# Reordering a dense unit: five products between uses of bank X, shrink's steps in three gaps, transforms in the first and fourth

## The chip, the cores and the metric

The kernel runs on one core of a Trainium2 chip. The metric is the device time in microseconds (us) of one execution, lower is better. All runs told of here are in the fast state (granted TensorE clock 0.984 to 0.99 over the span).

## The reference

```python
def _attn_ref(x, filt_r, filt_i):            # x (8, 3008, 256), filters (1505, 256)
    X = np.fft.rfft(x, axis=1)
    return np.fft.irfft(X * (filt_r + 1j * filt_i)[None], n=x.shape[1], axis=1)

def _moe_ref(x, w_in, w_out):                # x (24064, 256), w_in (256, 2048), w_out (2048, 256)
    h = x @ w_in
    return (h - np.tanh(h)) @ w_out
```

## The kernel before

The Fourier transforms are matrix products ("transforms": pf, pz, pe, pu), run for one batch while the dense layers of the batch before are computed. Each 2x2 block product of the dense layers is done with seven products and some sums in place of eight. The work is cut into 192 **dense units**, in five stages, 0 to 4, of 24, 48, 48, 48 and 24 units. Unit U runs three things at once: `up` of U (14 products into banks X, Y, Z), `shrink` of U-1 (the nonlinear part, on ScalarE and VectorE), and `down` of U-2 (14 products into four accumulator banks o0 to o3). The seven carry the numbers 1 to 7; each has two halves, and each half counts as one of the 14. Every fourth unit ends an accumulation, and `down` then also forms the output sums. There are four stretches between uses of bank X in a unit; I call them gaps one to four. In the program, `d()` issues `down`'s next products, `e()` its next sums, `s()` shrink's next step, `t(k)` one transform step if one is due.

```python
# up(U): the order of a unit
mm(X, 1, True); mm(Y, 2, True)
s1 = copied("s1")                            # ScalarE copies X
t(0); d(); s()
V.tensor_add(h[:, 0, :, 0:w], Y, s1)
e(); s(); s(); t(1)
mm(X, 6, False); mm(Z, 5, True)
u2 = copied("u2")
d(); s(); e(); t(2)
mm(X, 7, False)
u3 = copied("u3")
V.tensor_add(h[:, 3, :, 0:w], Z, u3)         # h3
d(); s(); e(); t(3)
mm(X, 4, False)
V.tensor_copy(h[:, 2, :, 0:w], X)            # h2: frees X for the next unit
s(); d(); e(); t(4)
mm(Z, 3, False)
V.tensor_add(h[:, 1, :, 0:w], Z, u2)

# shrink(U): 2 stands for h2 and h3, 0 for h0 and h1
def start(k):
    ACT.activation(y[k], ht[k], AF.Arctan, scale=S)
    ACT.activation(y[k], y[k], AF.Square)
def square(k):
    V.tensor_mul(ht[k], ht[k], y[k])
    ACT.activation(sq[k], y[k], AF.Square, bias=near_b, scale=A)
def end(k):
    V.scalar_tensor_tensor(out=ht[k], in0=sq[k], scalar=K, in1=ht[k], ...)
start(2); yield; square(2); yield; end(2); yield; start(0); yield; square(0); yield
end(0); combine(...)                         # four sums on GpSimd
yield

# down(U): two products share each accumulator bank
at = {1: (0, 0), 2: (0, 1), 3: (1, 0), 5: (1, 1), 6: (2, 0), 7: (2, 1), 4: (3, 0)}
mm(1, 2); yield                              # both halves k of both products
if done: ACT.copy(p1, product(1)); V.tensor_add(o[:, 0, 0:w], product(2), p1)
yield
mm(3, 5); yield
if done: ACT.copy(p5, product(5)); V.tensor_add(x12, product(3), p5)
yield
mm(6, 7); yield
if done: V.tensor_add(u2, product(6), p1); V.tensor_add(p1, product(7), u2); ...
yield
mm(4); yield
if done: ...
# ... (cut: transforms, loads and stores, weights, the exact fallback)
```

Of the kernel before, what the change touches and what calls it, by code (L numbers as in the profile page):

```python
# [143 lines left out]
def kernel(  # L144
# [9 lines left out]
    nc = tc.nc  # L154
    V, G, ACT = nc.vector, nc.gpsimd, nc.scalar
# [13 lines left out]
    def dram(t, off, dims):  # L169
        return bass.AP(tensor=t, offset=off, ap=[list(d) for d in dims])  # L170
# [19 lines left out]
    wd = cst.tile([128, 7, DFF // 2], F32, name="wd")  # L190
# [271 lines left out]
    def combine(b, t, shared=False):  # L462
        G.tensor_sub(t[0], b[0][1], b[0][0])  # L463
        G.tensor_sub(t[1], b[1][1], t[0])  # L464
        (V if shared else G).tensor_sub(t[2], b[1][1], b[0][1])  # L465
        G.tensor_sub(t[3], t[1], b[1][0])  # L466
# [4 lines left out]
    def up(U, d, e, s, t):  # L471

        i, u = divmod(U, 4)
        b, tu, w = uts[i]
        rhs = [b[0][0], b[1][0], b[1][1], tu[:, 3, 0:w], tu[:, 0, 0:w], tu[:, 1, 0:w],
               tu[:, 2, 0:w]]
        banks = {k: ps.tile([128, 2, 256], F32, tag=k, bufs=1, name=k) for k in "xyz"}
        X, Y, Z = (banks[k][:, :, 0:w] for k in "xyz")
        h = dn.tile([128, 4, 2, 256], F32, tag="h", bufs=3, name="h")
        hs[U] = (h, w)  # L480

        def mm(bank, q, first):
            for k in range(2):
                nc.tensor.matmul(bank[:, k], wu[:, q - 1, (2 * u + k) * 128:(2 * u + k + 1) * 128],  # L484
                                 rhs[q - 1], start=(first and k == 0), stop=True,
                                 skip_group_check=True)

        def copied(tag):
            t = dn.tile([128, 2, 256], F32, tag=tag, bufs=1, name=tag)[:, :, 0:w]
            ACT.copy(t, X)  # L490
            return t


        mm(X, 1, True)
        mm(Y, 2, True)
        s1 = copied("s1")
        t(0)
        d()
        s()
        V.tensor_add(h[:, 0, :, 0:w], Y, s1)  # L500
        e()
        s()
        s()
        t(1)
        mm(X, 6, False)
        mm(Z, 5, True)
        u2 = copied("u2")
        d()
        s()
        e()  # L510
        t(2)
        mm(X, 7, False)
        u3 = copied("u3")
        V.tensor_add(h[:, 3, :, 0:w], Z, u3)
        d()
        s()
        e()
        t(3)
        mm(X, 4, False)
        V.tensor_copy(h[:, 2, :, 0:w], X)  # L520
        s()
        d()
        e()
        t(4)
        mm(Z, 3, False)
        V.tensor_add(h[:, 1, :, 0:w], Z, u2)

    def shrink(U):

        h, w = hs.pop(U)  # L530
        ht = {k: h[:, k:k + 2].rearrange("p a b n -> p (a b) n")[:, :, 0:w] for k in (0, 2)}

        def tiles(tag, bufs):
            return dn.tile([128, 4, 256], F32, tag=tag, bufs=bufs, name=tag)[:, :, 0:w]

        y, sq = {}, {}

        def start(k):
            y[k] = tiles("y", 2)
            ACT.activation(y[k], ht[k], AF.Arctan, scale=S)  # L540
            ACT.activation(y[k], y[k], AF.Square)  # L541

        def square(k):
            sq[k] = tiles("sq", 1)
# [4 lines that stand above are left out]
            V.scalar_tensor_tensor(out=ht[k], in0=sq[k], scalar=K, in1=ht[k],  # L549
                                   op0=ALU.add, op1=ALU.mult)  # L550

        start(2)
        yield
        square(2)
        yield
        end(2)
        yield
        start(0)
        yield
        square(0)  # L560
        yield
        end(0)
        t = dn.tile([128, 4, 2, 256], F32, tag="t", bufs=2, name="t")
        blocks = [[h[:, 2 * a + k, :, 0:w] for k in range(2)] for a in range(2)]
        combine(blocks, [t[:, k, :, 0:w] for k in range(4)], U + 1 == 4 * len(groups))
        gs[U] = (blocks, t, w)
        yield
# [3 lines left out]
    def down(U):  # L571


        i, u = divmod(U, 4)
        b, t, w = gs.pop(U)
        rhs = [b[0][0], b[1][0], b[1][1], t[:, 3, :, 0:w], t[:, 0, :, 0:w], t[:, 1, :, 0:w],
               t[:, 2, :, 0:w]]
        if u == 0:
            accs[i] = [ps.tile([128, 2, 256], F32, tag=f"o{k}", bufs=1, name=f"o{k}")
                       for k in range(4)]  # L580
        acc = accs[i]
        at = {1: (0, 0), 2: (0, 1), 3: (1, 0), 5: (1, 1), 6: (2, 0), 7: (2, 1), 4: (3, 0)}

        def product(q):
            bank, k = at[q]
            return acc[bank][:, k, 0:w]

        def mm(*qs):
            for k in range(2):
                for q in qs:  # L590
                    nc.tensor.matmul(product(q), wd[:, q - 1, (2 * u + k) * 128:  # L591
                                                    (2 * u + k + 1) * 128],
                                     rhs[q - 1][:, k], start=(u == 0 and k == 0 and q == qs[0]),
                                     stop=(u == 3 and k == 1), skip_group_check=True)

        done = u == 3
        if done:
            p1, p5, u2, x12 = (dn.tile([128, 256], F32, tag=k, bufs=1, name=k)[:, 0:w]
                               for k in ("p1", "p5", "pu2", "x12"))
            o = dn.tile([128, 2, CH * 128], F32, tag="o", bufs=1, name="o")  # L600
        mm(1, 2)
        yield
        if done:
            ACT.copy(p1, product(1))
            V.tensor_add(o[:, 0, 0:w], product(2), p1)
        yield
        mm(3, 5)
        yield
        if done:
            ACT.copy(p5, product(5))  # L610
            V.tensor_add(x12, product(3), p5)
        yield
        mm(6, 7)
        yield
        if done:
            V.tensor_add(u2, product(6), p1)
            V.tensor_add(p1, product(7), u2)
            G.tensor_add(o[:, 0, w:2 * w], u2, x12)
        yield
        mm(4)  # L620
        yield
        if done:
            V.tensor_add(o[:, 1, 0:w], product(4), p1)
            G.tensor_add(o[:, 1, w:2 * w], p1, p5)
            accs.pop(i)
            if i + 1 < len(groups):
                stores.append((i, o))
            else:
                store_last(i, o)
        yield  # L630
# [162 lines left out]
    with tc.tile_pool(name="tr", bufs=2) as tr:  # L793
        with tc.tile_pool(name="pro", bufs=1) as pro, \
# [103 lines left out]
            with tc.manual_schedule():  # L898
# [43 lines left out]
                for j in range(NK // 2):  # L942
# [7 lines left out]
                    for i in range(2):  # L950
                        k = (2 * j + i) % 4
# [26 lines left out]
        with tc.tile_pool(name="dn", bufs=2) as dn, \  # L978
# [34 lines left out]
            with tc.manual_schedule():  # L1013
# [3 lines left out]
                for U in range(total + 2):  # L1017
                    i, u = divmod(U, 4)
                    if U < total:
                        p, c = groups[i]  # L1020
                        if c == 0 and u == 0:
                            units = 4 * len(CHUNKS[p])
                            steps, done = [], 0 if p else EARLY
                            if p + 1 < len(UNITS):
                                n_f = len(chunks_of(UNITS[p + 1], XH))
                                n_m = 2 * NK // (3 - len(UNITS[p + 1]))
                                steps = [0.01 * units + 1.36 * units * (k - done) / (n_f - done)
                                         for k in range(n_f)]
# [16 lines left out]
                    def d():  # L1045

                        next(dw, None)

                    def e():

                        next(dw, None)

                    def s():

                        next(sh, None)

                    def t(k):


                        nonlocal ms, done  # L1060
                        if k == 2 and stores:
                            store(*stores.pop())
                        store_some(4)
                        if U >= total:
                            return
                        pos = 20 * c + 5 * u + k
                        if u == 3 and k in (0, 2) and i + 1 < len(groups):
                            next(lasts)
                        elif done < len(steps) and steps[done] <= pos:
                            if done < n_f:  # L1070
                                next(fs)
                            else:
                                next(ms)
                            done += 1
                            if done == n_f:
                                ms = middle(p + 1, z1)
                                next(ms)
                        if i == len(groups) - 1 and U + 2 < total and k != 1:
                            next(bounds)
                        if k in (0, 2, 4):  # L1080
                            next(late, None)
                        elif U > 0:
                            next(copies, None)
# [56 lines left out]
```

## Time and profile before

| | before |
|---|---|
| time | 2852.15 us, median of 5 runs (2849.91 to 2857.07) |
| TensorE busy | 96% of the span |
| VectorE, ScalarE, GpSimd busy | 70, 66, 61% |
| start losses of TensorE after the prologue | 98.9 us of 2730 |

The **start loss** is by how much a record on TensorE starts later than usual after the one before it, put down to the product that starts late. The prediction below works it out and shows the lines.

In the profile's lines PE is TensorE, PEld its weight loads, DVE VectorE, ACT ScalarE and POOL GpSimd; L514 is line 514 of the kernel. Shrink's `square` and `end` are L545 and L549 before, L547 and L551 after; h3 is L514 and L513, h2 L520 and L519.

### The profile page before, as it was taken

Reading aid. Unit: us, or ns where it says so; the run is one execution under the profiler, and the core shown is the slowest. Engines: PE = TensorE matmul, PEld = TensorE weight load, DVE = VectorE, ACT = ScalarE, POOL = GpSimd, SP = SyncE. Lnnn points to the kernel's source line nnn. Section 1 sums busy time; section 2 is a strip of 40 time slices with the busy share of each in tenths; the row PEclk is TensorE's granted clock in tenths of the full one; section 3 lists DMA queues with packets and bytes.
Section 4 is the critical chain, followed back from the end, with each engine's and each line's share of the span. In section 5 each row is a group of like instructions: output and inputs, shape, how many; then the busy total and the mean of one; then the engine's idle time right before and its main releaser. Section 6 shows DMA issues by size and latency. Waiting matters only on the chain.

```text
span 2850.8 us, 36441 instructions
## 1 busy us (share of the span) xinstructions
PE 2744.0 (96%) x12482; PEld 2276.7 (80%) x12482; DVE 1983.7 (70%) x2211; ACT 1871.5 (66%) x2450; POOL 1738.0 (61%) x1381
## 2 busy tenths in 40 slices
PE   5789999999999999999999999999999999999998
PEld 2567777888878887888877788788888888898887
DVE  4675666766766777766776777676687777777876
ACT  3655666666666666666666667666666666666665
POOL 4345777544677767644576776755466666555554
PEclk7989999999999999999999999999999999999999
DMA  9644443232223322132232223212222322111010
GB/s 265 190 152 118 113 113 92 60 93 84 73 67 80 85 73 59 41 98 78 67 99 67 70 71 83 53 39 68 58 65 62 78 55 57 30 19 25 16 22 16
DMA packets 324269, 217.53 MB, mean 76 GB/s; under 512 B 225037, under 2 KB 276485, under 8 KB 323882
## 3 DMA queue, kind: packets, MB, share of 16 engines
q1 hardware_dynamic: 269304, 160.36, 23.1%
q10 hardware_dynamic: 52818, 51.53, 6.0%
q0 software_dynamic: 1952, 3.22, 0.5%
q8 instruction: 100, 1.64, 0.2%
q14 instruction: 95, 0.78, 0.1%
HBM read 138.87 MB, written 79.17 MB: 76 GB/s over the span
## 4 chain that ended last, share of the span: by engine, by line
PE 77%; ACT 8%; DVE 6%; issue 3%; DMA 3%; POOL 1%; SPq 1%; ACTq 1%; DVEq 0%; POOLq 0%
PE o L591 31%; PE x L484 20%; PE z L484 9%; PE y L484 5%; PE pe L365 3%; PE pu L448 3%; PE pz L384 3%; ACT y L540 2%; PE pf L305 2%; DVE h L545 2%; ACT y L541 1%; DVE uv L399 1%; ACT zs L398 1%; ACT u L490 1%; DMA filt<-in_filt_i_dram 1%
## 5 line engine op out<-in xcount | busy, mean ns | idle before, releaser
L591 PE MATMUL o<-t,wd 128*128 128x256 f32 (+2 forms) x3072 | 775.8, 375 | 0.0
L545 DVE TENSOR_TENSOR h<-h,y 128x1024 f32<-128x1024 f32 (+2 forms) x384 | 582.1, 1516 | 258.1 <-ACT y L541 258.1
L591 PEld LDWEIGHTS o<-t,wd 128*128 128x128 f32 x3072 | 580.6, 190 | 71.7
L484 PE MATMUL x<-tu,wu 128*128 128x256 f32 (+2 forms) x2304 | 591.6, 379 | 18.4 <-ACT u L490 16.9
L549 DVE SCALAR_TENSOR_TENSOR h<-sq,h 128x1024 f32<-128x1024 f32 (+2 forms) x384 | 569.9, 1484 | 20.8 <-ACT y L540 0.5
L463 POOL TENSOR_TENSOR t<-h 128x512 f32<-128x512 f32 (+2 forms) x192 | 240.7, 1253 | 558.9 <-DVE h L549 495.9
L591 PE MATMUL o<-h,wd 128*128 128x256 f32 (+2 forms) x2304 | 581.1, 375 | 0.2 <-DVE h L549 0.2
L484 PEld LDWEIGHTS x<-tu,wu 128*128 128x128 f32 x2304 | 429.4, 191 | 161.5 <-issue 73.3
L591 PEld LDWEIGHTS o<-h,wd 128*128 128x128 f32 x2304 | 430.9, 190 | 70.9 <-issue 19.1
L546 ACT ACTIVATE sq<-y,near_b 128x1024 f32<-128x1024 f32 (+2 forms) x384 | 435.4, 1134 | 6.1 <-DVE h L549 1.4
L540 ACT ACTIVATE y<-h 128x1024 f32<-128x1024 f32 (+2 forms) x384 | 400.0, 1042 | 14.8 <-ACT e L368 7.6
L541 ACT ACTIVATE y<-y 128x1024 f32<-128x1024 f32 (+2 forms) x384 | 399.3, 1040 | 12.2
L490 ACT COPY s<-x 128x512 f32<-128x512 f32 (+2 forms) x192 | 110.8, 577 | 439.8 <-PE x L484 431.2
L466 POOL TENSOR_TENSOR t<-t,h 128x512 f32<-128x512 f32 (+2 forms) x192 | 308.8, 1608 | 0.1
L490 ACT COPY u<-x 128x512 f32<-128x512 f32 (+2 forms) x384 | 219.4, 571 | 68.6 <-PE x L484 33.3
L464 POOL TENSOR_TENSOR t<-h,t 128x512 f32<-128x512 f32 (+2 forms) x192 | 241.7, 1259 | 15.1
L465 POOL TENSOR_TENSOR t<-h 128x512 f32<-128x512 f32 (+2 forms) x191 | 250.2, 1310 | 0.0
L400 POOL TENSOR_TENSOR zs<-zs,ft 128x512 f32<-128x512 f32 x112 | 165.9, 1481 | 117.4 <-ACT zs L398 117.3
L401 POOL TENSOR_TENSOR uv<-uv,zs 128x512 f32<-128x512 f32 x112 | 214.9, 1919 | 15.6 <-DVE uv L399 7.2
L484 PE MATMUL x<-ut,wu 128*128 128x256 f32 (+2 forms) x768 | 198.8, 381 | 8.1 <-DVE h L520 6.5
L500 DVE TENSOR_TENSOR h<-y,s 128x512 f32<-128x512 f32 (+2 forms) x192 | 130.2, 678 | 96.2 <-PE y L484 86.0
L484 PE MATMUL z<-tu,wu 128*128 128x256 f32 (+2 forms) x768 | 194.5, 376 | 0.1
(120 smaller groups left out, 3289.1 us busy)
## 6 DMA issues: line engine op xcount, KB each, us to landing
a<-ct SPq DMA_DIRECT2D x64, 384.0 KB
ct<-e ACTq DMA_DIRECT2D x128, 192.0 KB
ft<-filt SPq DMA_DIRECT2D x96, 256.0 KB
out_dram<-ot SPq DMA_DIRECT2D x1392, 16.0 KB
ct<-a ACTq DMA_DIRECT2D x80, 256.0 KB
x_sb<-in_x_dram SPq DMA_DIRECT2D x69, 256.0 KB
e<-ct SPq DMA_DIRECT2D x33, 512.0 KB
fg<-fg SPq DMA_DIRECT2D x40, 392.0 KB
```

The source lines that it names most:

```text
L463: G.tensor_sub(t[0], b[0][1], b[0][0])
L464: G.tensor_sub(t[1], b[1][1], t[0])
L465: (V if shared else G).tensor_sub(t[2], b[1][1], b[0][1])
L466: G.tensor_sub(t[3], t[1], b[1][0])
L484: nc.tensor.matmul(bank[:, k], wu[:, q - 1, (2 * u + k) * 128:(2 * u + k + 1) * 128], rhs[q - 1], start=(first and k == 0), stop=True, ski ...
L490: ACT.copy(t, X)
L540: ACT.activation(y[k], ht[k], AF.Arctan, scale=S)
L541: ACT.activation(y[k], y[k], AF.Square)
L545: V.tensor_mul(ht[k], ht[k], y[k])
L546: ACT.activation(sq[k], y[k], AF.Square, bias=near_b, scale=A)
L549: V.scalar_tensor_tensor(out=ht[k], in0=sq[k], scalar=K, in1=ht[k], op0=ALU.add, op1=ALU.mult)
L591: nc.tensor.matmul(product(q), wd[:, q - 1, (2 * u + k) * 128: (2 * u + k + 1) * 128], rhs[q - 1][:, k], start=(u == 0 and k == 0 and q == ...
```

## The change

The intent: bank X is used four times a unit, with 6, 6, 4 and 4 products between the uses. The two short gaps made TensorE wait for the copies out of X. The change makes all four gaps five products long by cutting `down` into groups of 3, 3, 5 and 3, gives each gap its share of shrink, and from stage 1 on keeps transforms out of gaps two and three (but for one pu in every fourth unit), so that they don't stand before u2, u3 and h2. The core of the diff:

```diff
         mm(X, 1, True)
-        mm(Y, 2, True)
         s1 = copied("s1")
+        mm(Y, 2, True)
         t(0); d(); s()
         V.tensor_add(h[:, 0, :, 0:w], Y, s1)
         e()
-        s(); s(); t(1)
         mm(X, 6, False)
-        mm(Z, 5, True)
         u2 = copied("u2")
-        d(); s(); e(); t(2)
+        mm(Z, 5, True)
+        t(1); d(); s(); e()
         mm(X, 7, False)
         u3 = copied("u3")
         V.tensor_add(h[:, 3, :, 0:w], Z, u3)
-        d(); s(); e(); t(3)
+        t(2); d(); s(); e()
         mm(X, 4, False)
         V.tensor_copy(h[:, 2, :, 0:w], X)
-        s(); d(); e(); t(4)
+        t(3); s(); d(); e()
         mm(Z, 3, False)
         V.tensor_add(h[:, 1, :, 0:w], Z, u2)
+        t(4)
 # shrink (start(k) is cut into turn(k), the arctan, and power(k), the square)
-        start(2); yield; square(2); yield; end(2); yield; start(0); yield; square(0); yield
+        turn(2); power(2); yield
+        square(2); turn(0); yield
+        end(2); power(0); square(0); yield
         end(0); combine(...)
 # down
-        mm(1, 2); yield
+        mm((1, 0), (2, 0), (1, 1)); yield
         if done: ACT.copy(p1, product(1))
-                 V.tensor_add(o[:, 0, 0:w], product(2), p1)
         yield
-        mm(3, 5); yield
+        mm((2, 1), (3, 0), (3, 1)); yield
+        if done: V.tensor_add(o[:, 0, 0:w], product(2), p1)
+        yield
+        mm((5, 0), (6, 0), (5, 1), (6, 1), (7, 0)); yield
         if done: ACT.copy(p5, product(5))
+                 V.tensor_add(u2, product(6), p1)
                  V.tensor_add(x12, product(3), p5)
+                 G.tensor_add(o[:, 0, w:2 * w], u2, x12)
         yield
-        mm(6, 7); yield
-        if done: V.tensor_add(u2, product(6), p1); V.tensor_add(p1, product(7), u2); G.tensor_add(...)
-        yield
-        mm(4); yield
-        if done: ...
+        mm((7, 1), (4, 0), (4, 1)); yield
+        if done: V.tensor_add(p1, product(7), u2); ...
 # places of transforms
-        elif done < len(steps) and steps[done] <= pos:
+        elif (p == 0 or k in (0, 3, 4)) and done < len(steps) and steps[done] <= pos:
```

More of the change, by code (lines that the diff above doesn't have):

```diff
@@ L494, in up @@
         mm(X, 1, True)
+        s1 = copied("s1")
         mm(Y, 2, True)
-        s1 = copied("s1")
         t(0)
@@ L501, in up @@
         e()
-        s()
-        s()
-        t(1)
-        mm(X, 6, False)
-        mm(Z, 5, True)
-        u2 = copied("u2")
+        mm(X, 6, False)
+        u2 = copied("u2")
+        mm(Z, 5, True)
+        t(1)
         d()
@@ L510, in up @@
         e()
-        t(2)
         mm(X, 7, False)
@@ L514, in up @@
         V.tensor_add(h[:, 3, :, 0:w], Z, u3)
+        t(2)
         d()
@@ L517, in up @@
         e()
-        t(3)
         mm(X, 4, False)
         V.tensor_copy(h[:, 2, :, 0:w], X)
+        t(3)
         s()
@@ L523, in up @@
         e()
-        t(4)
         mm(Z, 3, False)
         V.tensor_add(h[:, 1, :, 0:w], Z, u2)
+        t(4)
     def shrink(U):
@@ L536, in shrink, with turn, power @@
         y, sq = {}, {}
-        def start(k):
+        def turn(k):
             y[k] = tiles("y", 2)
             ACT.activation(y[k], ht[k], AF.Arctan, scale=S)
+        def power(k):
             ACT.activation(y[k], y[k], AF.Square)
@@ L550, in end @@
                                    op0=ALU.add, op1=ALU.mult)
-        start(2)
+        turn(2)
+        power(2)
         yield
         square(2)
+        turn(0)
         yield
         end(2)
-        yield
-        start(0)
-        yield
+        power(0)
         square(0)
@@ L588, in mm @@
         def mm(*qs):
-            for k in range(2):
-                for q in qs:
-                    nc.tensor.matmul(product(q), wd[:, q - 1, (2 * u + k) * 128:
-                                                    (2 * u + k + 1) * 128],
-                                     rhs[q - 1][:, k], start=(u == 0 and k == 0 and q == qs[0]),
-                                     stop=(u == 3 and k == 1), skip_group_check=True)
+            for q, k in qs:
+                nc.tensor.matmul(product(q), wd[:, q - 1, (2 * u + k) * 128:(2 * u + k + 1) * 128],
+                                 rhs[q - 1][:, k],
+                                 start=(u == 0 and k == 0 and at[q][1] == 0),
+                                 stop=(u == 3 and k == 1), skip_group_check=True)
         done = u == 3
@@ L600, in down @@
             o = dn.tile([128, 2, CH * 128], F32, tag="o", bufs=1, name="o")
-        mm(1, 2)
+        mm((1, 0), (2, 0), (1, 1))
         yield
@@ L604, in down @@
             ACT.copy(p1, product(1))
+        yield
+        mm((2, 1), (3, 0), (3, 1))
+        yield
+        if done:
             V.tensor_add(o[:, 0, 0:w], product(2), p1)
         yield
-        mm(3, 5)
+        mm((5, 0), (6, 0), (5, 1), (6, 1), (7, 0))
         yield
@@ L610, in down @@
             ACT.copy(p5, product(5))
+            V.tensor_add(u2, product(6), p1)
             V.tensor_add(x12, product(3), p5)
+            G.tensor_add(o[:, 0, w:2 * w], u2, x12)
         yield
-        mm(6, 7)
+        mm((7, 1), (4, 0), (4, 1))
         yield
         if done:
-            V.tensor_add(u2, product(6), p1)
             V.tensor_add(p1, product(7), u2)
-            G.tensor_add(o[:, 0, w:2 * w], u2, x12)
-        yield
-        mm(4)
-        yield
-        if done:
             V.tensor_add(o[:, 1, 0:w], product(4), p1)
```

## The prediction

> **What bounds the kernel now.** I read the page first. TensorE is busy 96% of the span, the others 61 to 70%.
>
> ```profile
> span 2850.8 us, 36441 instructions
> PE 2744.0 (96%) x12482; PEld 2276.7 (80%) x12482; DVE 1983.7 (70%) x2211; ACT 1871.5 (66%) x2450; POOL 1738.0 (61%) x1381
> ```
>
> So only TensorE's pauses can be won. A busy share hides part of them, because an end is modelled and a late start is swallowed by the overlap. I therefore used starts. In the timeline at 1505 us:
>
> ```profile
> 1504.95 1.89 PE L591 MATMUL o<-h,wd 128*128 128x256 f32 x8
> ...
> 1506.68 1.03 PE L484 MATMUL x<-tu,wu 128*128 128x256 f32 x4
> ```
>
> Eight records take 1506.68 - 1504.95 = 1.73 us, 0.216 us each. A product (one 128x128 weight block on 256 columns) is two records, 0.432 us; a transform (pz, pe, pf, pu) takes 0.86 us. I took each record's start from the timeline, subtracted the usual step of the record before it (0.216 us at 256 columns, 0.428 at 512, 0.109 at 128), and summed what is left, the **loss**, by the product that starts late. A dense unit is 28 products; there are 192, in five stages (24, 48, 48, 48, 24 units), with the next batch's transforms between the products of the first four. By stage, with its start and end in us:
> - prologue, 0 to 121: 58 us lost, not touched by the change;
> - stage 0, 121 to 534: 56.3 us (pe 23.3; bank X 20.2; pf, waiting for a DMA, 7.1);
> - stages 1 and 2, to 1210 and 1885: 10.4 and 11.1 us (bank X 8.6 and 9.2);
> - stage 3, to 2524: 12.6 us (bank X about 10);
> - stage 4 and the end: 8.5 us (bank X about 5).
>
> From 121 us on that is 99 us, 3.5% of the span. The view of waits, which counts only idle between modelled ends, has the same names (columns: total us, times, longest):
>
> ```profile
> PE x L484 <- ACT u L490: 16.9, 13, 3.8
> PE pe L365 <- DVE uv L399: 13.5, 18, 2.6
> ...
> PE x L484 <- DVE h L520: 6.5, 13, 1.0
> ```
>
> Bank X holds four results in turn in each unit; ScalarE copies the first three (s1, u2, u3), VectorE the fourth (h2, L520), and TensorE may write again only then. A late u3:
>
> ```profile
> 1511.85 1.89 PE L591 MATMUL o<-t,wd 128*128 128x256 f32 x8
> ...
> 1512.39 0.60 ACT L397 ACTIVATE zs<-pz 64x512 f32<-64x512 f32 x1
> ...
> 1513.00 0.58 ACT L398 COPY zs<-pz 64x512 f32<-64x512 f32 x1
> 1513.60 0.59 ACT L490 COPY u<-x 128x512 f32<-128x512 f32 x1
> ...
> 1514.24 1.13 PE L484 MATMUL x<-tu,wu 128*128 128x256 f32 x4 [0.50 <-ACT u L490]
> ```
>
> The copy stands behind a transform's two ScalarE operations, issued before X's product; TensorE has only four products to fill the time and starts 1514.24 - (1511.85 + 1.73) = 0.66 us late. The late h2 is alike: VectorE's uv of a transform stands before it and itself waits for ScalarE.
>
> **What the Trainium skill says.** (1) "Perfetto Trace Analysis", Identifying the Most-Contended Engine: matmul busy share is no good measure of distance to the limit. Agrees: busy 96% leaves 4%, yet the pauses by starts are larger than idle (18.2 us of idle shown before pe, where the starts lose 23.3 in stage 0 alone). (2) "PSUM — Partial Sum Buffer", PSUM bank collisions: engines are kept apart by bank, reads against reads too. The trace agrees: uv waits for ScalarE's zs on the same pz (117.2 us of DVE waits), and pe waits for uv, since all transforms share one bank. (3) The same page, Engine vs sequencer instructions: ScalarE, VectorE and GpSimd queues are strict FIFO. That is the mechanism above. (4) "SBUF — State Buffer", Who interferes with whom: a VectorE operation with two SBUF inputs contends with GpSimd's reads. Agrees: L549 takes 1.21 us at 298.00, but 2.10 at 804.64 with GpSimd at work.
>
> **The change part by part.** Products, matmul sizes, ScalarE, VectorE and GpSimd operations and DMAs stay in number; only order moves. So the 2,609 us of stream that I count from 150 to 2840 us stay.
>
> *Spacing of X.* Before, between uses of X: 6, 6, 4, 4 products; after, 5, 5, 5, 5. The two short gaps, X7 to X4 and X4 to the next X1, go from 4 x 0.432 = 1.73 us to 2.16. Nearly all X loss of stages 1 to 3 is theirs (x4, x1), in waits of 0.2 to 0.7 us.
>
> *Transforms.* From stage 1 on they stand at three places: in the first gap, and twice in the fourth, after h2 is issued. So from there on u2, u3 and h2 no longer stand behind a transform, but for one pu in every fourth unit. In the program order of both kernels I count only 5 of 48 units in stages 1 and 2 without a transform in the fourth gap, 11 in stage 3, 23 of 24 in stage 4. Each gives 0.86 us more of slack before X1.
>
> *Shrink.* ScalarE gets 0.59+1.06+1.06 = 2.7 us in gap one, 0.58+1.15+1.06 = 2.8 in gap two, 0.58+1.06+1.15 = 2.8 in gap three, against 7 x 0.432 = 3.02 of TensorE: it fits. But VectorE has more ahead of h2 than before: u3 lands 0.8 us after X7, then h3 (0.69), L549 (1.25 alone, 1.5 mean), L545 (1.22 alone, 1.5 mean), so h2 starts at 4.0 (alone) to 4.5 and ends at 4.7 to 5.2 us; X1 is due 12 products after X7, at 5.18. Without a transform in gap four that is the edge: I choose 0.15 us lost per such unit, and 0.7 where the unit also has output sums (every fourth).
>
> X then: stages 1 and 2 from about 9 to 2 us each; stage 3 from 10 to 3; stage 4 from 5 to 8 (18 x 0.15 + 6 x 0.7 is 6.9, rounded up).
>
> *What it costs: the transforms' bank.* Two transforms close together must wait for the bank:
>
> ```profile
> 294.40 1.02 PE L384 MATMUL pz<-a,fg 94*128 94x512 f32 x2
> ...
> 296.79 0.69 DVE L399 TENSOR_TENSOR uv<-pz,ft 128x512 f32<-128x512 f32 x1 [0.57 <-ACT zs L398]
> ...
> 297.63 1.07 PE L365 MATMUL pe<-uv,fg 112*96 112x512 f32 x2 [0.48 <-DVE uv L399]
> ```
>
> With four products between pz and pe, pe starts 297.63 - 294.40 - 0.86 - 1.73 = 0.64 us late, and that recurs unchanged through stage 0. With five it would be 0.64 - 0.43 = 0.21, with six none. In stages 1 and 2 the order before has 1 pz-to-pe spacing of four and none of five; after, 4 of four, 10 of five, and 3 pz-to-pu of four: 7 x 0.64 + 10 x 0.21 = 6.6 us per stage. That eats the 7 us gained. In stage 0 before there are 13 of four; after, 4 of four, 10 of five, 3 pz-to-pu of four: 8.3 becomes 6.6.
>
> *Stage 0.* The other 15 us of pe are five waits of 1.7 to 4.3 us behind crowded queues; I assume half stay (7). Of X's 20.2 us, 12.5 are four waits of 1.7 to 4.0 us in the first six units, where ScalarE's weight conversion waits for VectorE; copies now come ahead of it, but in all five places transforms stay in use. I choose 12. So 56 becomes 56 - 9 - 8 + 1 = 40.
>
> Sum of loss: 40 + 11 + 11 + 5 + 12 = 79 against 99: **20 us less, 2852 - 20 is about 2831.**
>
> **Rivals.** (a) *All X loss goes, and pe waits stay small*: 53 us of bank X and 9 of stage 0's pe won, less 13 for the new spacings, near 2803. For it: every X wait shown has one of the two mended causes. Against it: VectorE's longer list before h2. (b) *The wait moves*: h2 or L549 for the first down product (due 9 products, 3.89 us, after X4; h2, then L549, end at about 2.9 to 3.7, later with a pz in between) becomes the new pause in most units, 0.3 us x 192 = 58 us lost for 53 gained, near 2857. For it: the margin is 0.2 to 1.0 us. Against it: most units have another transform in gap four or one, 0.86 us each. (c) *GpSimd*: its four sums start later in the unit and a pz's uv behind them; before there was one such wait of 4.3 us. A few more in stage 0 would cost 5 to 10 us.
>
> **Range and chances.** 2852 - 2796 = 56 us, over half of all loss after the prologue, would be needed for 2%, more than all of bank X; a 2% loss would need all loss to grow by half. So almost surely within 2%. I take 2831, from 2803 (rival a) to 2856 (rival b).
>
> **What would show it.** Right: X waits on u2 and u3 nearly gone from stage 1 on; pe and pu waits on uv in stages 1 and 2 up from 1.8 to about 7 us a stage, at 0.2 and 0.64 us each; stage 1 no shorter than before by over 3 us; stage 3 shorter by 5 to 8; most of the gain in stage 0. Wrong: many o<-h waits on L549 in dense units (rival b), ScalarE lagging through all gaps, or stage 0 lengthened by GpSimd.

## More of the kernel before

In VectorE's waits one line of before matters later (columns: engine, result and line, what it waited for; total us, times, longest us):

```profile
DVE h L514 <- ACT u L490: 80.3, 67, 7.3
```

That is VectorE idle just ahead of h3, until ScalarE has copied u3.

## The result, and the profile after

| | before | after |
|---|---|---|
| median of 5 runs, us | 2852.15 | 2898.55 |
| lowest to highest | 2849.91 to 2857.07 | 2893.74 to 2904.63 |
| start losses after the prologue, us | 98.9 | 142.5 |

The ratio is 1.0162, 95% interval 1.0146 to 1.0178. A ratio is the mean time of one kernel's fast runs over that of the other's of the same rounds, so it is not quite the ratio of the medians. The kernel became 46 us slower, where 20 us less were predicted. The page after, its first lines:

```profile
span 2894.7 us, 36206 instructions
## 1 busy us (share of the span) xinstructions
PE 2751.4 (95%) x12482; PEld 2269.2 (78%) x12482; DVE 1907.6 (66%) x2211; ACT 1859.0 (64%) x2450; POOL 1727.5 (60%) x1381
```

The span grew by 43.9 us and the start losses by 43.6, so they account for the whole difference: TensorE does the same work and stands still longer. TensorE's waits after name new culprits:

```profile
PE o L592 <- DVE pu L616: 23.3, 31, 1.8
PE x L484 <- DVE h L519: 14.5, 23, 2.5
PE pe L365 <- DVE uv L399: 14.2, 23, 1.1
...
PE o L592 <- ACT p L605: 8.2, 15, 0.8
...
PE x L484 <- ACT u L490: 7.9, 4, 4.3
```

The first and the fourth line shown have no counterpart before: a product of `down` waits for the output sums. L616 is the sum that reads product 6, L605 the copy that reads product 1. By product, the start losses after the prologue are (us):

| late product | before | after |
|---|---|---|
| bank X (x1, x4, x6, x7) | 53.5 | 35.8 |
| pe and pu | 28.4 | 35.9 |
| second half of 7, every fourth unit | 0 | 38.1 |
| second half of 2, every fourth unit | 0 | 12.3 |
| all (the rest is in pf, pz, banks Y and Z, other o products and the end) | 98.9 | 142.5 |

One such unit in the last stage, where no transform is near (the timeline after; start us, length us, engine, line, operation, names, shape; TensorE, ScalarE, VectorE only):

```profile
2624.22 2.32 PE L592 MATMUL o<-t,wd 128*128 128x256 f32 x10
...
2625.04 0.69 DVE L513 TENSOR_TENSOR h<-z,u 128x512 f32<-128x512 f32 x1 [1.92 <-ACT u L490]
2625.65 1.21 DVE L551 SCALAR_TENSOR_TENSOR h<-sq,h 128x1024 f32<-128x1024 f32 x1
2626.38 1.03 PE L484 MATMUL x<-tu,wu 128*128 128x256 f32 x4
2626.78 1.22 DVE L547 TENSOR_TENSOR h<-h,y 128x1024 f32<-128x1024 f32 x1
2626.95 1.15 ACT L548 ACTIVATE sq<-y,near_b 128x1024 f32<-128x1024 f32 x1 [0.99 <-DVE h L551]
2627.91 0.41 DVE L616 TENSOR_TENSOR pu<-o,p 128x256 f32<-128x256 f32 x1
...
2628.38 1.56 PE L592 MATMUL o<-t,wd 128*128 128x256 f32 x6 [0.98 <-DVE pu L616]
...
2628.74 0.68 DVE L519 COPY h<-x 128x512 f32<-128x512 f32 x1
```

The five products of gap three start at 2624.22 and include both halves of product 6 and the first half of product 7, which share bank o2. Product 6 is ready, and its reader L616 is issued. But VectorE takes it only after h3, L551 (`end(2)`) and L547 (`square(0)`), at 2627.91. The second half of product 7 writes into the same bank, is due at 2626.38 + 0.86 = 2627.24 and starts at 2628.38, when the read is over: 1.14 us lost. Product 2's wait is of the same kind on ScalarE, in 15 of the 48 units with sums: its second half, due at 1519.19, starts at 1519.81, after L605, which ScalarE takes at 1519.40, behind a transform's copy and shrink's arctan and square (from 1516.37 on). Before h3, VectorE had idled for 1.92 us. Over the whole run that idle time is

```profile
DVE h L513 <- ACT u L490: 332.4, 187, 5.9
```

against 80.3 us before. VectorE, busy for less of the span than before, is idle in gap two and has a queue in gap three. The line of L548 shows ScalarE standing in that queue too (275.3 us over the run, waiting for L551).

### The profile page after: what moved, and what is told of

It is laid out like the page before. It is cut to its first block, busy times and chain, and to the rows that moved or that the text cites. A ratio compares the mean times of both kernels' runs of the same rounds, so it can differ in the third digit from the quotient of the medians.

```text
span 2894.7 us, 36206 instructions
## 1 busy us (share of the span) xinstructions
PE 2751.4 (95%) x12482; PEld 2269.2 (78%) x12482; DVE 1907.6 (66%) x2211; ACT 1859.0 (64%) x2450; POOL 1727.5 (60%) x1381
## 4 chain that ended last, share of the span: by engine, by line
PE 66%; DVE 13%; ACT 8%; DMA 4%; POOL 3%; issue 3%; SPq 1%; ACTq 0%; DVEq 0%; POOLq 0%
PE o L592 27%; PE x L484 17%; PE z L484 8%; PE y L484 4%; DVE h L551 4%; DVE h L547 3%; PE pu L448 3%; PE pe L365 3%; PE pz L384 2%; ACT u L490 2%; PE pf L305 2%; DVE h L513 1%; ACT y L540 1%; ACT zs L397 1%; ACT zs L398 1%
## 5 line engine op out<-in xcount | busy, mean ns | idle before, releaser
L547 DVE TENSOR_TENSOR h<-h,y 128x1024 f32<-128x1024 f32 (+2 forms) x384 | 584.9, 1523 | 325.0 <-ACT y L543 325.0
L592 PE MATMUL o<-t,wd 128*128 128x256 f32 (+2 forms) x3072 | 717.9, 376 | 25.3 <-DVE pu L616 23.3
L592 PEld LDWEIGHTS o<-t,wd 128*128 128x128 f32 x3072 | 571.2, 190 | 166.5 <-DVE pu L616 55.5
L548 ACT ACTIVATE sq<-y,near_b 128x1024 f32<-128x1024 f32 (+2 forms) x384 | 435.2, 1133 | 281.0 <-DVE h L551 275.3
L484 PE MATMUL x<-tu,wu 128*128 128x256 f32 (+2 forms) x2304 | 582.6, 375 | 9.3 <-ACT u L490 7.9
L592 PE MATMUL o<-h,wd 128*128 128x256 f32 (+2 forms) x2304 | 552.6, 376 | 10.5 <-ACT p L605 8.2
L551 DVE SCALAR_TENSOR_TENSOR h<-sq,h 128x1024 f32<-128x1024 f32 (+2 forms) x384 | 508.8, 1325 | 0.2
L540 ACT ACTIVATE y<-h 128x1024 f32<-128x1024 f32 (+2 forms) x384 | 397.3, 1035 | 14.1 <-ACT e L368 6.7
L513 DVE TENSOR_TENSOR h<-z,u 128x512 f32<-128x512 f32 (+2 forms) x192 | 130.5, 679 | 332.4 <-ACT u L490 332.4
L466 POOL TENSOR_TENSOR t<-t,h 128x512 f32<-128x512 f32 (+2 forms) x192 | 294.1, 1532 | 0.1
L400 POOL TENSOR_TENSOR zs<-zs,ft 128x512 f32<-128x512 f32 x112 | 154.2, 1376 | 150.3 <-ACT zs L398 150.1
L401 POOL TENSOR_TENSOR uv<-uv,zs 128x512 f32<-128x512 f32 x112 | 210.7, 1881 | 8.8
L484 PEld LDWEIGHTS x<-ut,wu 128*128 128x128 f32 x768 | 142.5, 191 | 80.3 <-DVE h L519 32.7
```

The costliest lines, as they stand in the source:

```text
L466: G.tensor_sub(t[3], t[1], b[1][0])
L484: nc.tensor.matmul(bank[:, k], wu[:, q - 1, (2 * u + k) * 128:(2 * u + k + 1) * 128], rhs[q - 1], start=(first and k == 0), stop=True, ski ...
L592: nc.tensor.matmul(product(q), wd[:, q - 1, (2 * u + k) * 128:(2 * u + k + 1) * 128], rhs[q - 1][:, k], start=(u == 0 and k == 0 and at[q] ...
```

## The experiments

My first theory (A) was the half-filled banks: with product groups cut across the two halves, a sum reads one product while the bank's other product is still to be finished. The rivals were that shrink's new grouping delays every reader, whatever the bank (B), and that the order of products is costly in itself (C). Each kernel was timed in three rounds beside the kernel before. The losses, in us, are those after the prologue, from one profile of each; "h2" is the median time from X4's last record to the start of h2's copy, from stage 1 on. Compare kernels by the ratios: the kernel before had medians of 2854.63 to 2855.12 us in the later rounds.

| kernel | median us | ratio to before | sums (7 and 2) | bank X | pe, pu | all losses | h2 |
|---|---|---|---|---|---|---|---|
| before | 2852.15 | 1 | 0 | 53.5 | 28.4 | 98.9 | 0.97 |
| after | 2898.55 | 1.0162 | 50.4 | 35.8 | 35.9 | 142.5 | 1.99 |
| reads_late | 2867.52 | 1.0049 | 0 | 46.3 | 43.4 | 113.5 | 2.07 |
| read_6_late | 2873.83 | 1.0071 | 12.0 | 43.4 | 40.3 | 121.0 | 1.99 |
| down_only | 2894.90 | 1.0145 | 36.8 | 52.9 | 32.6 | 139.6 | 0.76 |
| rest_only | 2933.17 | 1.0275 | 0 | 91.4 | 54.5 | 182.2 | 2.38 |
| sums_first | 2911.27 | 1.0204 | 13.2 | 67.3 | 48.7 | 156.2 | 2.21 |
| end2_early | 2821.55 | 0.9885 | 0 | 23.6 | 26.9 | 67.9 | 0.75 |
| slots_013 | 2904.82 | 1.0179 | 0 | 105.5 | 18.9 | 151.3 | 2.29 |
| end2_slots_013 | 2837.91 | 0.9952 | 0 | 51.2 | 14.1 | 83.6 | 1.20 |
| end2_only | 2842.19 | 0.9955 | 31.8 | 16.8 | 23.7 | 90.2 | 0.78 |
| rest_end2 | 2845.60 | 0.9963 | 0 | 32.5 | 38.5 | 89.6 | 1.27 |
| end2_slots_023 | 2816.19 | 0.9866 | 0 | 31.3 | 12.9 | 59.8 | 0.99 |
| end2_slots_all | 2833.22 | 0.9927 | 0 | 41.6 | 16.3 | 77.8 | 0.99 |

Every interval is the ratio plus or minus 0.002 or less. All outputs are right.

**reads_late**: each bank is read only when its last product is in.

```diff
         mm((1, 0), (2, 0), (1, 1)); yield
-        if done: ACT.copy(p1, product(1))
         yield
         mm((2, 1), (3, 0), (3, 1)); yield
-        if done: V.tensor_add(o[:, 0, 0:w], product(2), p1)
+        if done: ACT.copy(p1, product(1)); V.tensor_add(o[:, 0, 0:w], product(2), p1)
         ...
-                 V.tensor_add(u2, product(6), p1)          # gap three
         ...
+                 V.tensor_add(u2, product(6), p1)          # gap four, after (7, 1)
```

> The changed kernel, with the output sums of every fourth unit moved: product 1 is read one gap later and product 6 one gap later, so that each accumulator bank is read only when its last product is in. Theory (A, half-filled banks): the start losses of the products that follow those reads (7 second half 38.1 us, 2 second half 12.3 us, together 50.4 us) fall to under 5 us, and the time to 2843 to 2853 us, near or just under the kernel before. Rival (B, the regrouped shrink delays every reader on VectorE and ScalarE, whatever the bank): the losses move to other products and the time stays over 2880 us.

Measured: 2867.52 us, ratio 1.0049. The 50.4 us are gone, as A says, but the time fell by only 31 us: bank X lost 10.5 us more and pe and pu 7.5. The sum of product 6 now stands in gap four, and h2 is as late as before; 6.0 of the 8.6 us by which x1 grew stand at the X1 right behind the sums, which TensorE now reaches without having waited. So A is one cause and not the only one.

**read_6_late**: only product 6's read is moved.

> Only product 6's read is moved behind product 7's last write. Theory A: the 38.1 us of the second half of product 7 go, the 12.3 us of product 2 stay; time 2857 to 2867 us. Rival B: over 2880 us.

Measured: 2873.83 us. Product 7's 38.1 us are gone and product 2's 12.0 stay, each loss bound to its own read. The time is 7 us over the range, for the same reason as above.

**down_only**: the kernel before, with `down` alone replaced by that of the change.

> The kernel before with the changed kernel's down part alone (groups of 3, 3, 5 and 3 products, sums read where the change reads them); shrink and transforms as before. It also brings the spacing of five products. Theory A: product 7's second half again waits for the read of product 6, but VectorE has one operation less ahead of it, so I estimate 10 to 20 us lost there, under 5 us on product 2; bank X's 20 us on x4 mostly gone; time 2840 to 2865 us. Rival C (this order of products is costly by itself on TensorE, whatever the reads): losses spread over many o products of all units, time over 2880 us.

Measured: 2894.90 us, far over the range. Product 7 lost 25.3 us and product 2 11.5, so the new `down` brings those waits into the old order of shrink as well. But x4 hardly fell (20.0 to 18.6 us) and x7 rose from 11.6 to 28.7: with transforms and shrink where they were, the gap before x7 went from six products to five. Other o products lost under 7 us in all, which speaks against C. Why the sum for bank X didn't fall at all I have not followed copy by copy; that stays open.

**rest_only**: the changed kernel with `down` as before (4, 4, 4, 2).

> The changed kernel with the down part of the kernel before (groups 4, 4, 4, 2, each bank complete when read); shrink and transforms as changed. Theory A: o losses under 5 us; but pairs of transforms now stand four products apart where the change has five, so pe and pu lose some 10 to 12 us in each of stages 1 and 2, and bank X some 20 us more on x1; time 2855 to 2880 us. Rival B: o losses stay above 30 us and the time near or above 2898 us.

Measured: 2933.17 us. The sums' waits are gone, as complete banks demand; but x1 alone lost 81.2 us, where I had allowed for some 44, with h2 2.38 us after X4 and only four products to cover it. This is the first sign that the new shrink order (or the transforms' places, which came with it) is the larger fault: with it, both versions of `down` are slower than before.

**sums_first**: the changed kernel, with the sums of gap three issued ahead of shrink's step.

```diff
         t(2)
         d()
-        s()
         e()
+        s()
```

> The changed kernel, with the output sums of the third gap issued ahead of shrink's operations instead of behind them; the banks are read half filled as in the change. If the wait of product 7's second half (38.1 us) is the read's late place in VectorE's queue, it falls under 6 us, product 2's 12.3 us stay, and the time is 2862 to 2882 us, bank X's x1 a few us worse. If a half-filled bank costs whatever the place of the read, the 38 us stay and the time is near 2898 us.

Measured: 2911.27 us, outside the range and slower than the change. The wait of product 7 fell to 1.3 us though bank o2 is read half filled, so a half-filled bank costs only if its reader comes late. The time went into h2. A unit of the last stage again:

```profile
2637.58 1.03 PE L484 MATMUL x<-tu,wu 128*128 128x256 f32 x4
2637.78 0.42 DVE L616 TENSOR_TENSOR pu<-o,p 128x256 f32<-128x256 f32 x1 [0.85 <-PE o L592]
...
2638.45 1.22 DVE L551 SCALAR_TENSOR_TENSOR h<-sq,h 128x1024 f32<-128x1024 f32 x1
2639.59 1.75 DVE L547 TENSOR_TENSOR h<-h,y 128x1024 f32<-128x1024 f32 x1
...
2641.26 0.68 DVE L519 COPY h<-x 128x512 f32<-128x512 f32 x1
...
2641.99 0.48 PE L484 MATMUL x<-ut,wu 128*128 128x256 f32 x1 [1.23 <-DVE h L519]
```

The sum now starts as soon as product 6 is in, and product 7 runs on time. L551 and L547 come behind it, h2 behind them, and the next X1 waits. My theory had now to be changed: **gap three asks more of VectorE than it holds** (h3, L551, L547 and h2 take 3.8 us in the trace after, against 3.02 us of products from X7 to X4; in every fourth unit two sums come on top, in two others the work told of below), and which product waits only depends on what is last in the queue.

**end2_early**: reads_late, with `end(2)` moved to gap two, where VectorE idles.

```diff
         square(2)
         turn(0)
-        yield
         end(2)
+        yield
         power(0)
```

> The kernel with late reads, and shrink's last step for h2 and h3 (L549 of the kernel before) moved from the third gap into the second, where VectorE idles until u3. Theory: x1's 32.9 us come from h2 standing behind two shrink operations; with one of them gone x1 falls to 8 to 15 us, pe a little too (ScalarE's square no longer waits for that step); time 2835 to 2855 us. Rival: VectorE has no room in the second gap, h3 and u3 come late, x7 and x4 rise; time 2862 us or more.

Measured: 2821.55 us, ratio 0.9885, better than the range. h2 comes 0.75 us after X4 in place of 2.07, x1 falls from 32.9 to 7.1 us, and pe from 35.7 to 19.7: ScalarE's waits for L551, 281.6 us in reads_late, are gone, and the transforms' copies behind them come earlier. VectorE's idle time before h3 falls from 254.0 to 34.2 us.

**slots_013**: reads_late, with transforms in gaps one, two and four (once each).

```diff
-   elif (p == 0 or k in (0, 3, 4)) and ...
+   elif (p == 0 or k in (0, 1, 3)) and ...
```

> The kernel with late reads, and from stage 1 on transforms in gaps one, two and four instead of one and twice four: no pz-to-pe spacing under seven products in stages 1 and 2 (before this edit four of 4 and ten of 5). Theory: pe and pu, 27 us in stages 1 and 2, fall under 8 us; x1 or x7 gain up to 8 us as a transform now stands in the second gap before u3; time 2845 to 2862 us. Rival: the pe waits come from late ScalarE work, not from spacing, and stay over 20 us; time near 2867 us.

Measured: 2904.82 us. The spacing theory held for its own part, as pe lost next to nothing in stages 1 and 2. But x1 went to 84.9 us, 52 more where I had allowed for 8. As I read it, the second transform in gap four had been covering the late h2 by its 0.86 us.

**end2_slots_013**: both edits.

> Both edits. If they add up: x1 about 12 us, pe and pu about 25 us in all, time 2820 to 2842 us, under the kernel before. If the second gap now holds too much (L549 early and a transform): x7 and x4 over 15 us, time 2845 us or more.

Measured: 2837.91 us, inside the range, but by two misses that cancel: x1 keeps 30.2 us where 12 were expected, and pe and pu 14.1 where 25 were. It is 16 us over end2_early.

**end2_only**: the changed kernel with nothing but `end(2)` moved, as in end2_early.

> The changed kernel with one line moved: shrink's last step for h2 and h3 goes from the third gap into the second; the output sums stay where the change has them, reading half-filled banks. Theory (VectorE's queue in the third gap is what the change overfilled): product 7's 38.1 us fall under 15 us, as the read of product 6 has one operation less ahead; product 2's 12 us stay; x1's 24.3 us fall under 10; time 2838 to 2862 us. Rival (the half-filled banks are the cause by themselves): product 7 keeps over 25 us, time over 2865 us.

Measured: 2842.19 us, ratio 0.9955. One moved line makes the change faster than the kernel before. The same unit of the last stage as above:

```profile
2579.41 1.42 DVE L551 SCALAR_TENSOR_TENSOR h<-sq,h 128x1024 f32<-128x1024 f32 x1 [0.80 <-ACT sq L548]
...
2580.57 2.32 PE L592 MATMUL o<-t,wd 128*128 128x256 f32 x10
...
2581.39 0.69 DVE L513 TENSOR_TENSOR h<-z,u 128x512 f32<-128x512 f32 x1 [0.22 <-ACT u L490]
2582.34 1.22 DVE L547 TENSOR_TENSOR h<-h,y 128x1024 f32<-128x1024 f32 x1 [0.27 <-ACT y L543]
...
2583.49 0.41 DVE L616 TENSOR_TENSOR pu<-o,p 128x256 f32<-128x256 f32 x1
...
2583.95 1.35 PE L592 MATMUL o<-t,wd 128*128 128x256 f32 x5 [0.20 <-DVE pu L616]
```

L551 now ends before h3 can start, and the idle time before h3 is 0.22 us in place of 1.92. L616 starts 2583.49 - 2580.57 = 2.92 us after the products of gap three begin, in place of 3.69, and 7's loss in this unit is 2583.95 - 2580.57 - 2.16 - 0.86 = 0.36 us in place of 1.14. Over the run 7 keeps 20.0 us of 38.1, between the two forecasts (under 15, over 25), and 2 keeps 11.8, so the banks remain a second cause. x1 falls to 4.6 us.

**rest_end2**: `down` as before, with `end(2)` early.

> The down part of the kernel before (groups of 4, 4, 4, 2, so X's gaps are 6, 6, 4, 4 products), shrink and transforms as changed, and the early last step for h2 and h3. It tells what the five-product spacing is worth once VectorE's queue is right. Theory: x1's 81.2 us of the run without the early step fall under 20 us; pe stays at 10 to 16 us a stage, as transforms stand four products apart; time 2832 to 2855 us, over the 2821.6 us of the five-product version. Rival (spacing by itself matters more than the queue): x1 keeps over 40 us, time over 2870 us.

Measured: 2845.60 us. With the queue mended, x1 falls from 81.2 to 23.1 us, a little over the 20 expected. Against end2_only the five-product groups are worth nothing clear of noise (ratios 0.9963 and 0.9955, overlapping intervals; losses 89.6 and 90.2), since what bank X and pe gain (32.5 + 38.5 against 16.8 + 23.7) goes into the sums' waits (31.8). Against end2_early, whose sums come late, they are worth 22 us by the ratios.

**end2_slots_023** and **end2_slots_all**: end2_early with other places for transforms from stage 1 on, `k in (0, 2, 3)` and all five.

> Late reads and early step, transforms from stage 1 on in gaps one, three and four, at least seven products apart. If spacing of transforms were all: pe and pu of stages 1 and 2 from 15 to under 4 us, time 2808 to 2818 us. If VectorE's queue ahead of h2 rules: a transform's uv in the third gap stands there, x1 gains 15 to 30 us, time 2828 to 2850 us. I expect the second.

> Late reads and early step, and no restriction of the transforms' places at all. It tells what the restriction to the first and fourth gap is worth. Expected: pe and pu of stages 1 and 2 under 8 us, x1 and x4 together 15 to 30 us; time 2825 to 2845 us. If the restriction is worth nothing: 2815 to 2824 us.

Measured: 2816.19 us (ratio 0.9866, interval 0.985 to 0.9883) and 2833.22 us. I had expected the transform in gap three to hold up h2 by 15 us and more. It cost 9 (x1 7.1 to 16.0), and pe and pu gave back 14. end2_slots_all came as expected (x1 and x4 28.8 us together). The ratios of end2_early (0.9885, interval 0.9869 to 0.9902) and of end2_slots_023 come from different rounds and their intervals overlap, so which is better is not settled. Both beat the kernel before and the change. Of TensorE's waits in end2_slots_023 these are left for bank X and, after the prologue, for pe, and none for the sums:

```profile
PE x L484 <- DVE h L519: 9.1, 12, 2.6
...
PE x L484 <- ACT u L490: 6.8, 5, 2.9
PE x L484 <- ACT s L490: 3.7, 3, 2.4
PE pe L365 <- DVE uv L399: 3.4, 10, 0.7
```

The two causes of the slowdown together, as ratios to the kernel before:

| | `end(2)` in gap three (as changed) | `end(2)` in gap two |
|---|---|---|
| sums read half-filled banks (as changed) | 1.0162 | 0.9955 |
| sums read when the bank is complete | 1.0049 | 0.9885 |

Moving `end(2)` is worth 2.1 or 1.6%, reading late 1.1 or 0.7%. Either is worth less when the other is done; I take it that this is because both shorten the same queue.

## Why the prediction was wrong, point by point

- **The bound**, TensorE's start losses, held: they grew by 43.6 us and the span by 43.9. By stage they came to about 47, 26, 26, 22 and 22 us, where 40, 11, 11, 5 and 12 were predicted; only stage 0 became shorter, by 8.8 us.
- **The transforms' bank** held in its sum. pe and pu were put at about 7 us in each of stages 1 and 2 and came to 10.6. The spacing's part fits, since end2_only, with the same places, loses 6.7 there; the rest went when `end(2)` was moved, so I put it down to ScalarE's late copies. Stage 0 was put at 14 for pe; pe and pu there came to 14.2.
- **Bank X** went the right way, from 53.5 to 35.8 us, where the parts predicted make 12 + 2 + 2 + 3 + 8 = 27; by stage it was 16.8, 2.5, 2.8, 5.8 and 8.1. The copies u2 and u3 are no longer late after stage 0 (x4 and x7 lose 0.5 us in stages 1 to 4), and x1 keeps 24.3. That stages 1 to 4 came near the sizes is luck. Of the 18.1 us that x1 lost there, none stands behind the units with output sums, which were charged 0.7 us each: TensorE had already waited for the sums. All but 0.1 stands behind two kinds of unit whose extra work the prediction didn't list. The change moved `t(2)` from ahead of h3 to behind it, and with it two transposes of the output (L642, some 0.55 us each) in the unit after the sums, and a reduction of a transform's result (L453, 1.22 us) in the next. h2 was put at 4.0 to 4.5 us after X7's products. By median from stage 1 on it starts at 3.8 in plain units, 4.5 with sums, 4.9 behind L642 and 5.9 behind L453 (there X4 itself comes 0.9 us later). No run moved `t(2)` back by itself, so its own worth isn't known.
- **The step that failed is "Shrink"**, with "VectorE has more ahead of h2 than before". It saw the queue of gap three, but asked only what it does to h2, and charged the output sums to x1 as 0.7 us in every fourth unit. It did not see that these sums stand in the same queue and that TensorE waits for them. It had cited, under (2), that engines are kept apart by bank, and used this for the transforms' bank alone. The part that read the change's `down` counted products per gap and did not look at which bank each sum reads while which product is still to come: 0 us was put where 50.4 were lost. With the trace's own numbers it could have been worked out. From the last record of product 6 to the second half of 7 there are 0.216 + 0.43 + 0.86 = 1.51 us. The read takes 0.41 and a release some 0.05, so it must start within 1.05 us; behind h3, L551 and L547 it starts at 2.18 (median after), and 2.18 + 0.46 - 1.51 = 1.13 us is the loss shown above. Where a transform stands between (30 of the 48 units), 0.86 us less, 0.27. The next record is some 0.1 us late as well.
- **The rivals**: (a) and (c) did not happen. (b), a wait that moves, was the right kind in the wrong place: first `down` products behind h2 lost 5.2 us, not 58, while the sums, which no rival named, lost 50.4.
- **Gap two** was counted for ScalarE only, 2.8 us of 3.02. That VectorE idles there, 332 us in all, was not asked. It is what the cure rests on.
- **Smaller slips**: the + 1 in the sum for stage 0 isn't explained. And under (4) the two times of L549 don't set alone against together: at 298.00 GpSimd was at work too (L401, from 298.12, 2.21 us, where it takes 1.27 at 357.25). There VectorE had started first; at 804.64 GpSimd had (L466, from 803.41).

## What to carry to other kernels

When an order is planned gap by gap, fill in the table for every engine and for both sides of each wait: which queue does each reader of a bank stand in, what is ahead of it, and which product next writes that bank, also where only every fourth pass has such a reader. Ask too what a moved line brings along in some passes, as `t(2)` did. An engine that is idle on average in one gap and queued in the next may want one step moved forward, and that was worth more here than all the spacing of products. And when an experiment takes one wait away and the time does not follow, look at what is now last in the same queue.

## What the Trainium skill lacked or had wrong

- "Perfetto Trace Analysis", Matmuls, advises that independent groups rotate through PSUM banks so that one's evacuation overlaps the next one's products. It doesn't say what packing two products into one bank does to that. The passage that the prediction cites under (2) keeps engines apart by bank, which covers it, but neither gives a cost. Here a 0.41 us read of one half held up the other half's next product, 38.1 us over the run with the reader late and 1.3 us with it prompt.
- The same page's way to judge TensorE (load share in place of busy share) went the right way: 80% before, 78 after, 81 in the best kernel. So did the busy share (96, 95, 97). The page has no measure of pauses that adds up: the idle time between records (span less busy time) grew by 36.5 us, the differences of starts by 43.6, against 43.9 of span.
